# An FFT and two MLPs on one core: the steps from item 46 on in a new order, with subtractions split anew between VectorE and GpSimd

## The chip, the core and the metric

The kernel runs on one core of a Trainium2 chip. The metric is the time of one execution in device microseconds. The engines are named as a profile names them: PE (TensorE, the matrix engine, with PEld for its weight loads), DVE (VectorE), ACT (ScalarE), POOL (GpSimd) and SP (SyncE, which issues most DMAs). Each runs its own queue of instructions in order, and waits on semaphores for the others.

## What is computed

```python
X = np.fft.fft(np.fft.fft(x, axis=1), axis=2)      # x: 2 x 3008 x 256
x = X.real.reshape(6016, 256)
h = x @ w_in                                       # 256 x 2048
x = (h * np.clip(h + 3.0, 0.0, 6.0) / 6.0) @ w_out # 2048 x 256
xn = x / np.sqrt(np.mean(x * x, axis=-1, keepdims=True) + 1e-6) * rms_g
g = xn @ w_gate                                    # 256 x 1536
out = (g / (1 + np.exp(-g)) * (xn @ w_val)) @ w_out2   # 1536 x 256
```

All weights arrive as 64-bit floats, which the kernel decodes to 32 bits with integer operations.

## The kernel before

Every matrix product is made with operands split in two: `hi` is the 32-bit value rounded by ScalarE to the form that PE takes, `lo` is what is left, `f - hi`. A product is three passes (`PASSES`): hi x hi, and the two mixed ones. So each operand costs a copy on ScalarE and a subtraction, made by the helper `sub` (line 342). One helper for all of them means that all these subtractions have one line in the profile.

*First MLP.* The tokens are cut into six blocks of 2 x 502, the hidden units into 16 groups of 128; a block and a group make an **item**, 96 in all (`item1`). An item runs 6 matmuls into a pair of PSUM banks E and O (line 607, two pairs in turn), then on VectorE a multiply-add and two sums (lines 611, 613, 614), on ScalarE two ReLUs (619), on VectorE two multiplies (622), which read the banks for the last time, on ScalarE one rounding copy (625), two subtractions (342, `LO<-R,HI`), and 12 matmuls into four accumulators (640). The item two further on can start on the same pair of banks when line 622 has read them.

*Second MLP.* The same blocks, with 12 groups: 72 **chunks**. A chunk is seven products (`prod`, line 796, letters a to g in the order of steps), made by a scheme that saves one product in eight by sums and differences of the blocks of both operands; then on ScalarE copies from the bank (803), on VectorE sums with a bank (809), on ScalarE the SiLU (813), on VectorE the product of gate and value (817: of a tile with a bank, or of two tiles in SBUF, `R<-R,T`), a rounding copy (824), a subtraction (342), and the output matmuls (839).

*Work between.* While the first MLP runs, and into the second, the second MLP's weights are loaded (`load_w2`), decoded (`dec_w2`, lines 330 to 337: on VectorE two tensor_scalar and two operations on two tensors), summed (`sum_w2`, 711) and split (`split_w2`, 717 and 342). Each block is normalised (`rms`, 12 times): squares on ScalarE (739), their sum (742), a split, two matmuls with ones (751), a first guess by integer operations (755, 756), three Newton rounds (ScalarE 760, a product 762, VectorE 764) and two scalings (767). Its sums and differences (`sum_j`) and splits (`split_j`, 778) follow.

*The order.* It is written out by hand in one table, `STEPS` (from line 109 on). A word is a step: `47` is the next piece of item 47, `12d` the piece d of chunk 12, `rms5` the next piece of the sixth normalisation, and so on. Engines get their instructions in that order. Operations of `sub`, and lines 711, 742 and 762, go to GpSimd, and with an apostrophe behind the word to VectorE:

```python
        for step in STEPS.split():
            task = step.rstrip("'")
            low[0] = V if step != task else G
    def sub(o, a, b):
        low[0].tensor_tensor(o, a, b, op=ALU.subtract)
```

Of the kernel before, what the change touches and what calls it, by code (L numbers as in the profile page):

```python
# [132 lines left out]
    47 47 47 47 47 47 47 49 50 gr11 50 49 rms0 49 50 48 48 48 48 48 48 48 48 48 48 48 48 rms0 49' lo00 lo00 lo10 lo10 50  # L133
    gr11 rms0 gr11 gr11 gr11 gr11 rms0 pq11 51 51 50 pq11 pq11 pq11 pq11 pq11 rms0 51 49 49 49 49 49 49 49 49 rms0 51
    rms0 50 51 rms0 52 do00 50 rms0' 51 52 50 50 50 50 50 do10 52 51 52 rms0 51 52 53 rms0 rms0 53 52 51 51 51 51 53 52
    53 rms0 52 53 rms0 54 rms0 54 53 52 52 52 52 54 53 54 rms0 53 54 55 55 54 53 53 53 53 55 54 55 rms0 54 55 56 56 55
    54 54 54 54 56 55 56 do00 55 56 57 57 56 55 55 55 55 57 56 57 do00 56 do00 do00 58 57 hw07 lg00 lg00 56 56 56 56
    hw07 hw07 rms0 rms0 rms0 57 58 rms1 57 58 59 58 rms1 do10 58 dg00 57 57 57 57 57 rms1 59 58 rms1 59 59 rms1 58 do10
    59 rms1 58 58 58 58 58 rms1 59 do10 do10 rms1 59 60 dg00 lg10 lg10 hw08 60 rms1 61 60 60 59 59 59 59 59 rms1 60 hw08
    hw08 rms1 dg10 61 60 rms1 62 61 61 60 rms1 61 rms1 60 60 60 60 60 62 61 rms1 62 63 62 61 rms1 rms1 pq12 61 61 61 61  # L140
    61 rms1 rms1 rms1 62 pq12 pq12 pq12 pq12 pq12 63 64 62 63 62 hj00 63 64 62 62 62 62 62 63 hj01 hj00 hj00 64 63 65 64
    63 dg00 64 63 63 65 64 hj01 hj01 65 63 63 63 66 64 dg00 dg00 66 64 66 65 64 64 64 64 sj01 65 66 sj03 lv00 lv00 66 67
    65 hw00 65 67 68 66 67 65 65 65 65 65 hj04 68 66 68 67 66 66 66 66 66 67 dv00 hw00 hw00 dg10 67 dg10 68 69 67 dg10
    dg10 68 lv10 lv10 hw01 67 67 67 67 67 69 68 hw01 hw01 69 69 70 68 dv00 dv10 69 68 68 68 68 68 70 69 hj04 hj04 70 70
# [837 lines left out]
```

## Time and profile before

| | |
|---|---|
| median of 3 runs | 1093.73 us (1092.93 to 1095.08) |
| the profiled execution | 1095.86 us |
| its span, first to last instruction | 1094.1 us |
| PE busy | 1021.9 us (93%), 4356 matmuls recorded |
| DVE busy | 829.4 us (76%), 1202 instructions |
| ACT busy | 671.5 us (61%), 1081 |
| POOL busy | 616.1 us (56%), 500 |
| chain that ended last, by engine | PE 52%, DVE 37%, the rest 11% |
| mean granted clock of PE | 0.985 of 2.4 GHz |

The busy shares are means over stages with different limits. Matmuls are pipelined, so a matmul's own duration (some 390 ns) is longer than the time from its start to the next one's. The step at which the two orders part lies between items 47 and 51; item 50 starts at 289.1 us of the span, the second MLP's first output matmul at 519.1 us.

### The profile page before, as it was taken

What the parts mean: (1) busy time and instruction counts of PE and PEld (TensorE: products, weight loads), DVE (VectorE), ACT (ScalarE), POOL (GpSimd) and SP (SyncE); (2) the same over time, 40 slices, a digit from 0 to 9 for tenths busy, and PEclk for the clock granted to TensorE, in tenths of its full rate; (3) what the DMA queues carried; (4) which work ended last, traced back from release to release, by engine and by line L of the source; (5) the groups of instructions that cost most, each with busy time, mean ns of one, the idle gap of its engine ahead of it and who ended that gap; (6) DMA issues with size and microseconds to landing.
All of it is one profiled execution on the core that took longest, in us unless ns stands there. A gap on an engine that the chain in (4) does not pass through costs nothing.

```text
span 1094.1 us, 12459 instructions
## 1 busy us (share of the span) xinstructions
PE 1021.9 (93%) x4356; PEld 820.3 (75%) x4356; DVE 829.4 (76%) x1202; ACT 671.5 (61%) x1081; POOL 616.1 (56%) x500
## 2 busy tenths in 40 slices
PE   3879899999998899989988999999999999999997
PEld 2758777888875678768766777888788788878885
DVE  7998999987799999996798768556755755764443
ACT  5656556555656656666666666566566666755553
POOL 0057567666667869664656656636545753653332
PEclk9899999999999999999998999999999999999998
DMA  8450302043501110110130110110020011000001
GB/s 284 152 174 0 81 33 82 1 84 60 143 1 39 58 39 20 58 58 24 64 104 1 39 38 0 37 40 1 1 76 1 1 38 38 1 1 38 1 1 38
DMA packets 22118, 53.27 MB, mean 49 GB/s; under 512 B 4326, under 2 KB 9958, under 8 KB 21678
## 3 DMA queue, kind: packets, MB, share of 16 engines
q1 hardware_dynamic: 19320, 45.10, 12.5%
q0 software_dynamic: 2736, 7.38, 3.3%
q8 instruction: 34, 0.56, 0.2%
q14 instruction: 28, 0.23, 0.1%
HBM read 36.58 MB, written 11.32 MB: 44 GB/s over the span
## 4 chain that ended last, share of the span: by engine, by line
PE 52%; DVE 37%; issue 4%; ACT 3%; POOL 3%; DMA 1%; SPq 0%; POOLq 0%; DVEq 0%; ACTq 0%
PE E L796 13%; PE acc L839 13%; PE acc L640 10%; PE O L796 10%; DVE R L622 6%; DVE T L611 4%; DVE E L613 3%; DVE O L614 3%; PE E L607 2%; PE O L607 2%; DVE H L764 2%; DVE R L817 2%; DVE R L809 1%; DVE YB L335 1%; DMA J<-in_x 1%
## 5 line engine op out<-in xcount | busy, mean ns | idle before, releaser
L342 POOL TENSOR_TENSOR LO<-R,HI 128x502 fp32r<-128x502 f32 x191 | 246.1, 1313 | 132.5 <-ACT HI L625 128.5
L640 PE MATMUL acc<-HI,B 128*128 128x502 f32 x768 | 250.8, 392 | 0.6 <-ACT HI L625 0.3
L640 PEld LDWEIGHTS acc<-HI,B 128*128 128x128 f32 x768 | 145.7, 190 | 31.8 <-ACT HI L625 2.6
L640 PE MATMUL acc<-LO,B 128*128 128x502 f32 x384 | 153.6, 400 | 8.9 <-POOL LO L342 8.9
L342 POOL TENSOR_TENSOR HI<-R,HI 128x502 fp32r<-128x502 f32 x72 | 87.4, 1216 | 114.9 <-ACT HI L824 56.5
L625 ACT CAST HI<-R 128x1004 fp32r<-128x1004 f32 x96 | 99.2, 1036 | 85.6 <-DVE R L622 55.3
L809 DVE TENSOR_TENSOR R<-R,O 128x502 f32<-128x502 f32 x144 | 96.2, 674 | 49.6 <-PE O L796 39.3
L342 POOL TENSOR_TENSOR LO<-R,LO 128x502 fp32r<-128x502 f32 x68 | 82.6, 1218 | 87.8 <-ACT LO L824 48.3
L813 ACT ACTIVATE R<-R 128x502 f32<-128x502 f32 x144 | 89.7, 626 | 38.8 <-DVE R L809 38.2
L619 ACT ACTIVATE R<-E,c_three 128x502 f32<-128x502 f32 x96 | 65.3, 680 | 73.8 <-DVE E L613 59.4
L803 ACT COPY R<-E 128x502 f32<-128x502 f32 x144 | 83.0, 576 | 36.4 <-PE E L796 33.5
L607 PE MATMUL E<-J,A 128*128 128x502 f32 x288 | 84.9, 404 | 16.6 <-DVE R L622 13.8
L640 PEld LDWEIGHTS acc<-LO,B 128*128 128x128 f32 x384 | 72.9, 190 | 33.6 <-POOL LO L342 19.0
L809 DVE TENSOR_TENSOR T<-T,O 128x502 f32<-128x502 f32 x48 | 32.4, 675 | 71.6 <-ACT T L803 71.6
L607 PE MATMUL O<-J,A 128*128 128x502 f32 x288 | 83.4, 398 | 0.3 <-DVE A L390 0.3
L607 PEld LDWEIGHTS E<-J,A 128*128 128x128 f32 x288 | 54.6, 194 | 33.1 <-DVE R L622 19.6
L613 DVE TENSOR_TENSOR E<-T,O 128x502 f32<-128x502 f32 x96 | 65.6, 684 | 8.2
L622 DVE SCALAR_TENSOR_TENSOR R<-R,E 128x502 f32<-128x502 f32 x96 | 64.3, 669 | 3.6 <-ACT R L619 3.5
L614 DVE TENSOR_TENSOR O<-T,O 128x502 f32<-128x502 f32 x96 | 65.1, 678 | 0.0
L607 PEld LDWEIGHTS O<-J,A 128*128 128x128 f32 x288 | 55.5, 193 | 12.4 <-DVE A L390 0.7
L619 ACT ACTIVATE R<-O,c_three 128x502 f32<-128x502 f32 x96 | 64.7, 674 | 0.0
L622 DVE SCALAR_TENSOR_TENSOR R<-R,O 128x502 f32<-128x502 f32 x96 | 64.1, 668 | 0.0
(354 smaller groups left out, 2237.7 us busy)
## 6 DMA issues: line engine op xcount, KB each, us to landing
out_dram<-H SPq DMA_DIRECT2D x22, 251.0 KB, 2.0
y<-H SPq DMA_DIRECT2D x10, 502.0 KB, 2.8
W<-y SPq DMA_DIRECT2D x20, 251.0 KB, 2.8
A<-in_w_in SPq DMA_DIRECT2D x4, 1024.0 KB, 9.1
W<-in_w_out SPq DMA_DIRECT2D x6, 512.0 KB, 3.4
W<-in_w_gate SPq DMA_DIRECT2D x6, 512.0 KB, 3.5
W<-in_w_val SPq DMA_DIRECT2D x6, 512.0 KB
PQ<-in_x SPq DMA_DIRECT2D x3, 1008.0 KB
```

What stands on the lines that cost most here:

```text
L342: low[0].tensor_tensor(o, a, b, op=ALU.subtract)
L607: T.matmul(bk[:, :BL], a[:, lw, eo, fs], j[:, eo, lx], start=(n == 0), stop=(n == 2))
L613: V.tensor_tensor(E[:, :BL], t, O[:, :BL], op=ALU.add)
L614: V.tensor_tensor(O[:, :BL], t, O[:, :BL], op=ALU.subtract)
L619: S.activation(x, bk[:, :BL], AF.Relu, bias=c3)
L622: V.scalar_tensor_tensor(x, x, 6.0, bk[:, :BL], op0=ALU.min, op1=ALU.mult)
L625: S.copy(hi, r.rearrange("p (h n) -> p h n", h=2))
L640: T.matmul(acc[k][:, :BL], w[:, lw, f % 4, d * P:(d + 1) * P], (hi, lo)[lx][:, hf], start=(first and n == 0), stop=(last and n == 2))
L796: T.matmul(bk[:, :BL], w[:, lw, fs], j[:, lx], start=(n == 0 and m in (0, 1, 3)), stop=(n == 2), skip_group_check=True)
L809: V.tensor_tensor(c["t"][m], c["t"][m], c["b", 1][:, :BL], op=ALU.add)
L813: S.activation(t, t, AF.Silu)
L839: T.matmul(acc2[p, m][d][:, :BL], w[:, lw, cs], h[:, lx], start=(f == 0 and n == 0), stop=(f == NF2 - 1 and n == 2))
```

## The change

Only the table `STEPS` differs, and in it only the words from item 46's surroundings on; the words ahead of them are the same. The new words are the same steps in a new order, with apostrophes at other places. Two lines of the 109 that differ:

```diff
@@ -130,109 +130,109 @@
...
-    47 47 47 47 47 47 47 49 50 gr11 50 49 rms0 49 50 48 48 48 48 48 48 48 48 48 48 48 48 rms0 49' lo00 lo00 lo10 lo10 50
-    gr11 rms0 gr11 gr11 gr11 gr11 rms0 pq11 51 51 50 pq11 pq11 pq11 pq11 pq11 rms0 51 49 49 49 49 49 49 49 49 rms0 51
...
+    47 47 47 47 47 47 47 49 50 48 48 48 48 48 48 48 48 48 48 48 48 49 50 49 50 50 49 gr11 lo00 lo00 50 lo10 lo10 rms0 50
+    rms0' 51 gr11 50 rms0 gr11 gr11 gr11 gr11 pq11 49 49 49 49 49 49 49 49 rms0' 51 do00 pq11 pq11 pq11 pq11 pq11 51 51
...
```

In the built program every engine has the same operations as before, except that 76 instructions stand on VectorE's queue that stood on GpSimd's: 43 of line 342, 18 of line 762, 12 of line 742 and 3 of line 711.

What moved is seen at three places. First VectorE's queue in the first MLP, around item 73, where a part of `w_gate` is decoded into tile B (T, E, O and R are the item's tiles; X and c_wx its inputs; W the raw weights). Before:

```order
L611 SCALAR_TENSOR_TENSOR T_627_3357<-X_9_81,c_wx_77,E_624_3331 128x502
L613 TENSOR_TENSOR E_624_3331<-T_627_3357,O_625_3332 128x502
L614 TENSOR_TENSOR O_625_3332<-T_627_3357,O_625_3332 128x502
L332 TENSOR_SCALAR B_488_2559<-B_488_2559 128x512
L333 TENSOR_SCALAR B_488_2559<-B_488_2559 128x512
L622 SCALAR_TENSOR_TENSOR R_630_3365<-R_630_3365,E_624_3331 128x502
L622 SCALAR_TENSOR_TENSOR R_630_3365<-R_630_3365,O_625_3332 128x502
L611 SCALAR_TENSOR_TENSOR T_633_3393<-X_9_81,c_wx_77,E_631_3368 128x502
L613 TENSOR_TENSOR E_631_3368<-T_633_3393,O_632_3369 128x502
L614 TENSOR_TENSOR O_632_3369<-T_633_3393,O_632_3369 128x502
L335 SCALAR_TENSOR_TENSOR B_488_2559<-W_607_3230,B_488_2559 128x512
L622 SCALAR_TENSOR_TENSOR R_638_3409<-R_638_3409,E_631_3368 128x502
```

Now:

```order
L622 SCALAR_TENSOR_TENSOR R_620_3306<-R_620_3306,E_615_3277 128x502
L622 SCALAR_TENSOR_TENSOR R_620_3306<-R_620_3306,O_616_3278 128x502
L332 TENSOR_SCALAR B_483_2536<-B_483_2536 128x512
L333 TENSOR_SCALAR B_483_2536<-B_483_2536 128x512
L611 SCALAR_TENSOR_TENSOR T_624_3324<-X_9_81,c_wx_77,E_621_3312 128x502
L613 TENSOR_TENSOR E_621_3312<-T_624_3324,O_622_3313 128x502
L614 TENSOR_TENSOR O_622_3313<-T_624_3324,O_622_3313 128x502
L622 SCALAR_TENSOR_TENSOR R_626_3342<-R_626_3342,E_621_3312 128x502
L622 SCALAR_TENSOR_TENSOR R_626_3342<-R_626_3342,O_622_3313 128x502
L335 SCALAR_TENSOR_TENSOR B_483_2536<-W_595_3163,B_483_2536 128x512
L332 TENSOR_SCALAR B_483_2536<-B_483_2536 128x512
L333 TENSOR_SCALAR B_483_2536<-B_483_2536 128x512
```

Lines 332 and 333, and 335, stood between line 614 and the two lines 622 of the same item; they now stand behind the second line 622, ahead of line 611 of the next item.

Second, VectorE's queue in the second MLP's first chunks, where weights are decoded into tile YB (R, T and c_p are the chunks' tiles, E and O the banks, B and A the split weights). Before:

```order
L809 TENSOR_TENSOR T_824_4502<-T_824_4502,O_821_4472 128x502
L817 TENSOR_TENSOR R_823_4501<-R_823_4501,E_819_4459 128x502
L809 TENSOR_TENSOR R_828_4542<-R_828_4542,O_832_4555 128x502
L332 TENSOR_SCALAR YB_826_4515<-YB_826_4515 128x512
L333 TENSOR_SCALAR YB_826_4515<-YB_826_4515 128x512
L335 SCALAR_TENSOR_TENSOR YB_826_4515<-W_830_4547,YB_826_4515 128x512
L337 SCALAR_TENSOR_TENSOR YB_826_4515<-W_830_4547,YB_826_4515 128x512
L332 TENSOR_SCALAR YB_826_4515<-YB_826_4515 128x512
L333 TENSOR_SCALAR YB_826_4515<-YB_826_4515 128x512
L335 SCALAR_TENSOR_TENSOR YB_826_4515<-W_833_4570,YB_826_4515 128x512
L337 SCALAR_TENSOR_TENSOR YB_826_4515<-W_833_4570,YB_826_4515 128x512
L809 TENSOR_TENSOR R_823_4501<-R_823_4501,O_821_4472 128x502
```

Now:

```order
L809 TENSOR_TENSOR T_822_4474<-T_822_4474,O_825_4510 128x502
L817 TENSOR_TENSOR R_821_4473<-R_821_4473,E_820_4465 128x502
L337 SCALAR_TENSOR_TENSOR YB_823_4493<-W_813_4421,YB_823_4493 128x512
L809 TENSOR_TENSOR R_832_4567<-R_832_4567,O_831_4562 128x502
L332 TENSOR_SCALAR YB_823_4493<-YB_823_4493 128x512
L333 TENSOR_SCALAR YB_823_4493<-YB_823_4493 128x512
L809 TENSOR_TENSOR R_821_4473<-R_821_4473,O_825_4510 128x502
L335 SCALAR_TENSOR_TENSOR YB_823_4493<-W_827_4538,YB_823_4493 128x512
L342 TENSOR_TENSOR B_828_4540<-YB_823_4493,B_828_4540 128x512
L337 SCALAR_TENSOR_TENSOR YB_823_4493<-W_827_4538,YB_823_4493 128x512
L817 TENSOR_TENSOR R_821_4473<-R_821_4473,T_822_4474 128x502
L332 TENSOR_SCALAR YB_823_4493<-YB_823_4493 128x512
```

The four decoding operations stood in runs of four and eight; they now stand singly or in pairs between the chunks' lines 809 and 817, with a weight's subtraction (342) among them that was on GpSimd.

Third, a normalisation in the second MLP's steady part (H holds the value and its inverse root, HI the product of a Newton round). Before, GpSimd's queue:

```order
L342 TENSOR_TENSOR PQ_567_3023<-H_1025_6136,PQ_567_3023 128x502
L342 TENSOR_TENSOR LO_1027_6173<-R_1016_6060,LO_1027_6173 128x502
L342 TENSOR_TENSOR LO_1031_6203<-R_1016_6060,LO_1031_6203 128x502
L342 TENSOR_TENSOR PQ_567_3023<-W_974_5750,PQ_567_3023 128x502
L762 TENSOR_TENSOR HI_1030_6196<-HI_1030_6196,H_1025_6136 128x502
L342 TENSOR_TENSOR HI_1034_6230<-R_1022_6130,HI_1034_6230 128x502
L762 TENSOR_TENSOR HI_1030_6196<-HI_1030_6196,H_1025_6136 128x502
L342 TENSOR_TENSOR HI_1037_6261<-R_1022_6130,HI_1037_6261 128x502
L342 TENSOR_TENSOR W_974_5750<-W_976_5778,W_974_5750 128x502
```

Now the rounds on VectorE's queue:

```order
L756 TENSOR_SCALAR H_1019_6107<-H_1019_6107 128x502
L762 TENSOR_TENSOR HI_1030_6198<-HI_1030_6198,H_1019_6107 128x502
L809 TENSOR_TENSOR T_1025_6142<-T_1025_6142,O_1023_6130 128x502
L764 SCALAR_TENSOR_TENSOR H_1019_6107<-HI_1030_6198,H_1019_6107 128x502
L809 TENSOR_TENSOR R_1033_6214<-R_1033_6214,O_1032_6208 128x502
L762 TENSOR_TENSOR HI_1030_6198<-HI_1030_6198,H_1019_6107 128x502
L817 TENSOR_TENSOR R_1024_6141<-R_1024_6141,E_1022_6123 128x502
L764 SCALAR_TENSOR_TENSOR H_1019_6107<-HI_1030_6198,H_1019_6107 128x502
L809 TENSOR_TENSOR R_1024_6141<-R_1024_6141,O_1023_6130 128x502
L762 TENSOR_TENSOR HI_1030_6198<-HI_1030_6198,H_1019_6107 128x502
L817 TENSOR_TENSOR R_1024_6141<-R_1024_6141,T_1025_6142 128x502
L764 SCALAR_TENSOR_TENSOR H_1019_6107<-HI_1030_6198,H_1019_6107 128x502
```

Two of this normalisation's three products (762) stood on GpSimd, whose result line 764 on VectorE takes; now all three stand on VectorE.

## Rows read from the trace of the kernel before

**Rows 1.** Four stretches: us, busy us (instructions) by engine, granted clock, DMA share, GB/s

```profile
289.10:519.10 230.00, 215.48 (x914) 168.36 (x913) 213.46 (x311) 146.39 (x212) 161.52 (x125) 1.00 0.13 44
519.10:632.00 112.90, 101.23 (x410) 78.01 (x409) 93.40 (x119) 71.70 (x131) 70.89 (x54) 0.95 0.17 56
632.00:1004.40 372.40, 367.32 (x1592) 297.71 (x1592) 231.35 (x315) 239.65 (x429) 202.22 (x168) 1.00 0.06 20
1004.40:1094.10 89.70, 83.46 (x358) 67.43 (x356) 37.96 (x58) 44.56 (x77) 26.96 (x23) 0.96 0.05 18
```

**Rows 2.** The same view: a piece of the first stretch, and one without waits

```profile
300.00:400.00 100.00, 89.68 (x372) 67.80 (x371) 97.64 (x135) 60.56 (x88) 74.13 (x58) 1.00 0.10 32
...
1000.00:1050.00 50.00, 50.00 (x222) 41.37 (x221) 23.69 (x36) 28.04 (x49) 15.41 (x13) 1.00 0.03 11
```

**Rows 3.** Single lines on VectorE: count, shortest/median/longest ns, first and last start

```profile
L764 DVE SCALAR_TENSOR_TENSOR H<-HI,H x30: 667/682/1754, 580.8 to 958.9; 128x502 f32<-128x502 f32 x30
...
L622 DVE SCALAR_TENSOR_TENSOR R<-R,E x96: 659/670/680, 54.9 to 504.1; 128x502 f32<-128x502 f32 x96
...
L335 DVE SCALAR_TENSOR_TENSOR YB<-W,YB x12: 682/694/1740, 455.9 to 566.0; 128x512 int32<-128x512 int32 x12
...
L333 DVE TENSOR_SCALAR YB<-YB x12: 426/427/1490, 455.4 to 565.1; 128x512 int32<-128x512 int32 x12
```

**Rows 4.** Order of time, VectorE then GpSimd: start us, us, instruction, idle time before

```profile
317.87 0.68 DVE L614 TENSOR_TENSOR O<-T,O 128x502 f32<-128x502 f32 x1
318.45 1.15 DVE L767 SCALAR_TENSOR_TENSOR YB<-YB,c_gn,HI 128x502 f32<-128x502 f32 x1
...
342.86 0.68 DVE L337 SCALAR_TENSOR_TENSOR B<-W,B 128x512 int32<-128x512 int32 x1
343.46 1.50 DVE L332 TENSOR_SCALAR B<-B 128x512 f32<-128x512 f32 x1
...
317.79 2.75 POOL L342 TENSOR_TENSOR LO<-R,HI 128x502 fp32r<-128x502 f32 x2 [1.50 <-ACT HI L625]
...
343.30 1.38 POOL L342 TENSOR_TENSOR LO<-R,HI 128x502 fp32r<-128x502 f32 x1 [1.39 <-ACT HI L625]
```

**Rows 5.** Groups on VectorE, 289.1 to 519.1: count, busy us, mean ns

```profile
L337 DVE SCALAR_TENSOR_TENSOR B<-W,B 128x512 int32<-128x512 int32 x6 | 7.6, 1267 | 0.1
L764 DVE SCALAR_TENSOR_TENSOR HI<-R,HI 128x502 f32<-128x502 f32 x6 | 6.8, 1131 | 0.0
L767 DVE SCALAR_TENSOR_TENSOR YB<-YB,c_gn,HI 128x502 f32<-128x502 f32 x4 | 6.6, 1670 | 0.0
L335 DVE SCALAR_TENSOR_TENSOR B<-W,B 128x512 int32<-128x512 int32 x6 | 6.6, 1100 | 0.0
L333 DVE TENSOR_SCALAR B<-B 128x512 int32<-128x512 int32 x6 | 6.5, 1088 | 0.2
L332 DVE TENSOR_SCALAR B<-B 128x512 f32<-128x512 f32 x6 | 5.6, 932 | 0.0
```

**Rows 6.** Order of time: VectorE from 357.61, TensorE's wait at 362.23

```profile
357.61 3.98 DVE L767 SCALAR_TENSOR_TENSOR YB<-YB,c_gn,HI 128x502 f32<-128x502 f32 x2
...
362.23 0.96 PE L607 MATMUL E<-J,A 128*128 128x502 f32 x3 [2.26 <-DVE R L622]
```

**Rows 7.** Order of time, TensorE, 554 to 561 us

```profile
554.15 0.85 PE L796 MATMUL E<-J,B 128*128 128x502 f32 x3
...
558.12 1.17 PE L796 MATMUL O<-PQ,A 128*128 128x502 f32 x3 [2.44 <-DVE R L809]
559.08 1.46 PE L796 MATMUL O<-B,B 128*128 128x502 f32 x3
```

**Rows 8.** Groups on VectorE, 632.0 to 1004.4; then TensorE at 774.90 us

```profile
L817 DVE TENSOR_TENSOR R<-R,T 128x502 f32<-128x502 f32 x33 | 28.3, 861 | 16.2 <-ACT R L813 15.7
L764 DVE SCALAR_TENSOR_TENSOR H<-HI,H 128x502 f32<-128x502 f32 x24 | 26.5, 1106 | 7.0 <-POOL HI L762 6.4
...
774.90 0.95 PE L796 MATMUL O<-YB,B 128*128 128x502 f32 x3 [0.49 <-DVE T L809]
```

More of the change, by code (lines that the diff above doesn't have):

```diff
@@ new lines @@
+    dv12 dv12 6u hw25 rms2 ly1 ly1 7e rms2 hw25' hw25 6w 7l rms2 sw21' rms2 7f sw23' hw23 8a sw22' hw24 8b hw23' hw23
+    hw22 sw24' 8h hw22' hw22 hw26 8c hw24' hw24 8k hw26' hw26 8e rms2' 7m 8l rms2 7g 7n rms2 8f 7o 7r rms2 9a 8i 7p 9b
+    9h 7q 8d 8j 7s 9i 7t 9c 8m 9j 7v 7u 8n 9k 8r rms2 7w 8s rms2 rms2' 8g rms2 9d 8o 9e rms2 8p 8v rms2 rms2 rms2 9l
+    hj10 8q 9f rms3 9m hj10 hj10 10a 9n 8t 9g rms3' 9r 8u 10b 10h 9o rms3 10c 10i 9s 9p 8w 10j rms3' 10k 9q rms3 hj11
+    10d rms3 hj11' hj11 10e 9t rms3 9v 10l 9u rms3 10m 10f rms3' 9w rms3 10n rms3 10g 10r rms3' 11a 10s 10o 11b 10p rms3
@@ new lines @@
+    10v 11h 10q rms3 11i 10t rms3 11c 11j 11d 11k 10u 12a 10w rms3 12h rms3 rms3 rms3 rms3 11e sj11' 12b hj16 sj13' 11l
+    hj13 hj16' hj16 11f hj14 11m hj13 hj13 11n 11g hj14' hj14 11r 13a 11o sj12 13h 12i 13b 11s 11p 12d hj12 13i 12j 11v
+    sj14' 13j hj12' hj12 hj15 11q 12c ev0o0 hj15' hj15 11t 13c ev0o0 ev0o0 12k ly2 11u 13d ly2 ly2 13k 12e 11w 12l 12m
+    ev0o0 ev0o0 12f 12g 12n 13e 12o 12r 14a 12p 12s 14b 13l 14h 12q 13f ev0o1 13m 12v 12t ev0o1 ev0o1 12u 13n 13g 14i
+    13r 12w 13o 14j 13s 13p ev0o1 ev0o1 14c 13q 14d 13t 13v 14k 13u rms4 13w rms4' 14e rms4 15a 14l rms4' 15b 15h 14m
@@ new lines @@
+    24j 22v 22u 23o 23r 23p 23s 22w 23q 24c 23t 24d 24k 23u 23v ev1o0 23w ev1o0 ev1o0 24e 25a 24l 25b 24m 25h ev1o0
+    ev1o0 24f 25i 24g 24n 25j 25c 24o 24r 25d 24p 24s 26a ev1o1 25k 24q 24v ev1o1 26h ev1o1 24t 25e 24u 26c 25l 24w 25m
+    ev1o1 ev1o1 26k 25f 25g 25n 26b 25o 25r 26e rms6 26i 25s 27a 25p rms6' 26d 26j 25q 25v rms6 25t rms6' 26l 25u 27b
+    27h 26m 26f 27i 25w 26n 27j 26r 26g 26s 27c 26o 27d 26p rms6 27k 26q 26v rms6 26t rms6 27e 26u rms6 28a 27l rms6'
+    26w 28h 27m rms6 27f rms6 27g 27n rms6 28c 27o 27r 28b 27p 27s 29a 28k 28i 28e rms6 28j 27q 28d 29h rms6 27v 27t
@@ new lines @@
+    32n 32g 31u hj32 32r 33b 32o sj34 33h 31w 32p 33i 32s 33j 33c 32q 33d 33k hj32' hj32 32t 32v 32u 33e 32w 33l 33m 33f
+    33g 33n 34a 33o 33r 34b 33p 33s 35a 34h 33q 34c 35h 34i 33v 33t 34k 33u 34j 34d hj34 33w hj34' hj34 34e 35c 34l 35b
+    34m 35k hj36 34f 35i hj35 hj36 hj36 34g 34n 35j 35d 34o 34r hj35 hj35 35e 34p 36a 34s ly4 35l ly4 ly4 36b 35m 36h
+    35f 34q 36i 35g 34t 35n 36j 34v 34u 35o 35r 35p 35s 34w 35q 36c 35t 36d 36k 35u 35v ev2o0 35w ev2o0 ev2o0 36e 37a
+    36l 37b 36m 37h ev2o0 ev2o0 36f 37i 36g 36n 37j 37c 36o 36r 37d 36p 36s 38a ev2o1 37k 36q 36v ev2o1 38h ev2o1 36t
@@ new lines @@
+    41o 42d 41p rms9 42k 41q 41v hj41 rms9 hj41' hj41 41t rms9 42e 43a 41u rms9 43b 42l rms9' 43h 41w 42m rms9 43i 42f
+    rms9 43j 42g rms9' 42n 43c rms9 42r 43d 42o 43k 42s 44a rms9 43e 42p rms9' 44h 42v 42q 43l rms9 42t 43f 43m 42u 44c
+    43n 42w rms9 43r 44k rms9 rms9 rms9 43s 43g 44b 43o 44e sj41' 43p 43v 44i hj43 sj43 44l 43q 44j 44d hj43' hj43 43t
+    44f 44m sj42 45a 44n 44g 43u hj42 44r 45b 44o sj44 45h 43w 44p 45i 44s 45j 45c 44q 45d 45k hj42' hj42 44t 44v 44u
+    45e 44w 45l 45m 45f 45g 45n 46a 45o 45r 46b 45p 45s 47a 46h 45q 46c 47h 46i 45v 45t 46k 45u 46j 46d hj44 45w hj44'
@@ L236 @@
+    71q 71t ev5o0 71u ev5o0 ev5o0 71w ev5o1 ev5o0 ev5o0 ev5o1 ev5o1 ev5o1 ev5o1
 """
```

176 lines of the change are left out of this document (75 added, 101 removed).

## The prediction

> **What bounds the kernel now.** I read the stretches first, then what the engines wait for, then the order of the instructions.
>
> The span after item 50 falls into four stretches, one row each [rows 1]: the rest of the first MLP (289.1 to 519.1 us), the first twelve chunks of the second MLP with the last of the weight decoding (519.1 to 632.0), its steady part (632.0 to 1004.4) and the end. Where nothing holds TensorE up it runs 222 matmuls in 50.00 us [rows 2], 0.2252 us each. At that pace the four stretches need 914 x 0.2252 = 205.8, 410 x 0.2252 = 92.3, 1592 x 0.2252 = 358.5 and 358 x 0.2252 = 80.6 us. They took 230.0, 112.9, 372.4 and 89.7. So 24.2, 20.6, 13.9 and 9.1 us are waiting, 68 us in all; no reordering can give back more than that.
>
> In the first stretch the engine that sets the pace is VectorE: 97.64 busy of 100 us in one piece of it [rows 2], where PE stands at 89.68. Part of that busy time is no work. A multiply that takes one operand from PSUM (L622) lasts 659 to 680 ns whatever else runs. An operation with both inputs in SBUF lasts 667 ns at its shortest, but up to 1754 (L764); L335 goes from 682 to 1740, and L333, a tensor_scalar from SBUF to SBUF, from 426 to 1490 [rows 3]. The rows in order of time say when: the L767 of 318.45 takes 1.15 us while GpSimd works on two low-word subtractions from 317.79 on; the L337 of 342.86, which GpSimd does not meet, takes 0.68, and the L332 behind it, which runs into the GpSimd subtraction of 343.30, takes 1.50 [rows 4]. In the first stretch six groups carry most of this [rows 5]. Against the shortest durations, and about 0.7 for L767, it is 6 x 0.585 + 6 x 0.464 + 4 x 0.95 + 6 x 0.418 + 6 x 0.66 + 6 x 0.51 = 19.6 us; with the smaller groups of the same view some 27. The same sum gives some 24 us in the second stretch and 32 in the third.
>
> What it costs TensorE is seen where the slow instruction stands between the sum that ends an item's pre-activation (L614) and the multiply that frees its PSUM banks (L622). Two L767 at 357.61 took 3.98 us there, and TensorE waited 2.26 us for that L622 [rows 6].
>
> **The change part by part.** It is a permutation: the same 4358 matmuls, 1083 ScalarE and 113 SyncE instructions. 76 instructions leave GpSimd for VectorE: 43 subtractions (L342), 18 products (L762), 12 sums (L742) and 3 sums (L711), counted in the two orders. By stretch that is 3, 25 and 48.
>
> *Their price.* A VectorE instruction follows the one before by 0.6 us (317.87 to 318.45) [rows 4], so 2, 15 and 29 us of VectorE. On GpSimd they took some 1.3 us each (2.75 for two [rows 4]); GpSimd has room either way.
>
> *First stretch.* Of the runs of SBUF-only operations between items on VectorE, 30 of 41 stood right behind an L614 before, which is when GpSimd subtracts for the item ahead [rows 4]; now 14 of 42 do, 23 stand right behind the second L622, where GpSimd still waits for ScalarE's rounding, and 5 elsewhere. I take half of the 27 us as gone, since half of the runs have left the place where they collide: 13.5 us, less 2 for the three added, plus something for the L622s that are no longer held. **-13 us.** Ends: -24, when TensorE runs at its pace throughout, and 0, when the new places collide as the old ones did. If this stall goes, the next late thing is TensorE itself; the margin left is 11 us.
>
> *Second stretch.* VectorE is busy 93.4 of 112.9 us [rows 1]: 69.7 of work, 23.7 of collision. With 15 added it has 84.7 of work against TensorE's 92.3. GpSimd is busy 70.9 us, 63% of the stretch; without 25 operations of 1.3 it has 39, 37% of some 105. Collisions in proportion to that, on 93 exposed operations where 68 were, are 23.7 x 37/63 x 93/68 = 19 us. The order also avoids some, as in the first stretch; I take 13. VectorE then needs 98. It stood idle for 19.5 us, mostly behind chunks whose own sums it had delayed: it ran decoding in runs of eight, and TensorE waited 2.44 us for an L809 behind one. After that wait the matmuls ran at the lower of the clock's two levels, 1.2 GHz: 1.46 us for three from 559.08 on, where three took 0.85 before [rows 7], so 0.6 us lost on each such group; the granted clock of the stretch is 0.95 [rows 1]. The new order deals the decoding out in ones and twos between the chunk's operations; I leave 8 us idle. 98 + 8 = 106, **-7 us.** Ends: -20 (TensorE's pace), and +15, if the collisions stay at 24 and the idle time at 19.5 (84.7 + 24 + 19.5 = 128).
>
> *Third stretch.* Here VectorE has room: 231.4 of 372.4 us, 260 with the 29. The waits are short and come with each normalisation: L764, the last step of a Newton round, at 1106 ns where it needs 667, 24 times; the product with both inputs in SBUF at 861, 33 times; and TensorE's wait for the L809 behind them, 0.49 us at 774.90 [rows 8], which comes back in each two blocks. In a Newton round the product (L762) used to cross to GpSimd and back; now it stands on VectorE in most rounds and GpSimd is not in the chain. I take a little under half of the 13.9 us. **-6 us.** Ends: -14, and +5 if each of five normalisations gains a new wait of 1 us because VectorE has become the later engine.
>
> *End.* The last chunks' subtractions stay on GpSimd, and its low words are the last thing the final matmuls wait for. **0**, ends -1 and +1.
>
> *DMAs.* The weight loads and the reloads of the first MLP's output move with their steps on SyncE's queue, each still a few items or chunk operations ahead of its first reader; none of the waits named here goes to such a load. 0.
>
> The sum is -26 us against the profiled execution's 1095.86: 1069.9. That execution stands 2.1 us above the median of the runs, 1093.73, so the forecast for the median is **1068 us**.
>
> One rule of the Trainium skill goes further than the rows. "SBUF — State Buffer", section Who interferes with whom, has the two engines' shared port pair as an exclusive lock that whoever starts first holds for the whole instruction. The durations in rows 3 and 4 agree with it. By that rule alone a right order avoids every collision, all 83 us of VectorE time would go, and the sum would be the low ends, -59 us, near 1036. I don't take it, since 14 of 42 runs still stand at the old place.
>
> **Rivals.**
>
> *A. VectorE becomes the bound in the second stretch (slower).* It gets 25 more operations just where decoding, splitting and the chunks meet. If each of the 93 exposed operations collides as the 68 do now (23.7 / 68 = 0.35 us), that is 32 us, and 84.7 + 32 + 8 = 125, +12. An order that is wrong about the collisions there is wrong elsewhere: -6 in the first stretch, +4 in the third. Sum +10, 1104 us. It decides from the point at which collisions there pass 112.9 - 84.7 - 8 = 20 us. For it: VectorE is the fullest engine behind TensorE. Against it: GpSimd has half as much to collide with. Chance 0.14.
>
> The Trainium skill speaks for A: "Perfetto Trace Analysis", section Optimizing Scalar/DVE Operations, would move work off a saturated VectorE, even to GpSimd, which is the reverse of this change; it adds that between these two engines it might not help.
>
> *B. The change doesn't do what it says.* The places on VectorE are new, but GpSimd's turn shifts with them, and each collision is met one item later. Then only what is moved counts, the 2 to 3 us of both signs cancel, and the time is 1093. For it: queues run free of any clock, so that an order only fixes who follows whom on one engine. Against it: the place behind L622 is tied to GpSimd's wait by data, not by timing. Chance 0.06.
>
> *C. Only the first stretch gains.* 13 us there, nothing elsewhere: 1081. For it: VectorE is nearly full in the second stretch before and after. Chance 0.15, and the forecast's case has 0.65.
>
> **How the numbers follow.** A measurement of this kernel tells 0.2% (2.2 us) from no change. Faster by more: forecast and C, 0.80. Within 0.2%: B, 0.06. Slower: A, 0.14. The range holds the forecast and C: its low end, 1050, is the forecast with three quarters of the way to the low ends in the first two stretches (0.75 x 24 = 18), its high end, 1090, is C with the second and third stretches worse by 9 together. It leaves out A, and half of B's case.
>
> **What would show it.** Right: in the first stretch L335, L337 and L764 at means under 0.9 us, DVE's busy share near 0.95 with PE at 0.96 or more, and a length of 214 to 220 us; in the second stretch GpSimd busy about 40 us and no piece at the lower clock; in the third a PE wait of under 1 us in each two blocks. Wrong: VectorE over 98 busy of the second stretch's length with PE waiting for L809 or L817; or L764 and L337 at their old means, which is B.

## The result, and the profile after

The changed kernel takes **1066.24 us** (median of 4 runs, 1064.86 to 1067.67), the kernel before 1094.40 in the same comparison: a ratio of 0.9744, 95% interval 0.9726 to 0.9763, 2.6% faster. The forecast was 1068 and the range 1050 to 1090.

The same stretches as in [rows 1], in the trace after (us, then busy us and instructions of PE, PEld, DVE, ACT and POOL, granted clock, DMA share, GB/s):

```profile
286.90:502.20 215.30, 209.80 (x912) 170.28 (x911) 197.13 (x314) 145.28 (x213) 149.05 (x120) 1.00 0.14 45
502.20:605.90 103.70, 99.03 (x411) 76.25 (x410) 91.78 (x142) 72.48 (x131) 38.84 (x30) 0.98 0.20 64
605.90:972.80 366.90, 365.90 (x1593) 297.43 (x1591) 243.80 (x364) 236.04 (x427) 141.04 (x120) 1.00 0.06 20
972.80:1063.80 91.00, 84.30 (x361) 66.80 (x359) 43.34 (x58) 44.66 (x78) 27.12 (x24) 0.99 0.05 18
```

The span went from 1094.1 to 1063.8, 30.3 us: 14.7 in the first stretch, 9.2 in the second, 5.5 in the third, -1.3 in the end, and 2.2 ahead of item 50. That last one is not the change's: the steps there are the same, and in the runs below that leave them as they are they took between 285.8 and 289.6.

VectorE has 76 instructions more and is no busier, 829.7 us where it was 829.4. The groups of [rows 5], on VectorE in the first stretch after (count, busy us, mean ns, idle time before):

```profile
L335 DVE SCALAR_TENSOR_TENSOR B<-W,B 128x512 int32<-128x512 int32 x6 | 4.2, 701 | 0.0
L337 DVE SCALAR_TENSOR_TENSOR B<-W,B 128x512 int32<-128x512 int32 x6 | 4.2, 700 | 0.0
L764 DVE SCALAR_TENSOR_TENSOR HI<-R,HI 128x502 f32<-128x502 f32 x6 | 4.1, 675 | 0.0
...
L333 DVE TENSOR_SCALAR B<-B 128x512 int32<-128x512 int32 x6 | 2.6, 428 | 0.2
L332 DVE TENSOR_SCALAR B<-B 128x512 f32<-128x512 f32 x6 | 2.5, 420 | 0.0
```

L337 went from 1267 ns to 700, L764 from 1131 to 675, L333 from 1088 to 428, close to the shortest times of [rows 3].

Adding up what every VectorE instruction with all its operands in SBUF (the lines listed below, 755, 756, and 817 with two tiles) takes above its clean duration (L764 676 ns, L335 and L337 691, L333 427, L332 418 and so on for the other lines) gives the **excess** of a stretch, the measure used from here on. It fell from 27.9 to 8.8 us in the first stretch, from 23.6 to 8.8 in the second, from 32.3 to 16.8 in the third; in the end it rose from 0.1 to 4.9.

Why it fell is seen where the two engines meet. For the SBUF-only instructions of VectorE in the first stretch (lines 332, 333, 335, 337, 342, 711, 742, 762, 764, 767), I asked whether a GpSimd instruction ran alongside, and which of the two had started first. "Long" is over 0.1 us above the shortest of the same line and shape in the run:

| | no GpSimd alongside | VectorE first | GpSimd first |
|---|---|---|---|
| before | 11, 0 long | 6, 0 long | 46, 44 long, 26.0 us above |
| after | 27, 0 long | 13, 0 long | 28, 16 long, 7.4 us above |

Where VectorE starts first, it isn't slowed. Where GpSimd is first, VectorE's instruction ends only after GpSimd's. Before, in order of time, VectorE and then GpSimd:

```profile
404.08 0.82 DVE L332 TENSOR_SCALAR B<-B 128x512 f32<-128x512 f32 x1
404.94 1.18 DVE L333 TENSOR_SCALAR B<-B 128x512 int32<-128x512 int32 x1
...
403.35 2.49 POOL L342 TENSOR_TENSOR LO<-R,HI 128x502 fp32r<-128x502 f32 x2 [1.44 <-ACT HI L625]
```

GpSimd's two subtractions end at about 404.6 and at 405.84. L332 ends at 404.90 and L333 at 406.12, each some 0.28 us behind one of them. An L337 of 0.68 us, met in the same way, ends 0.55 us behind GpSimd's first:

```profile
413.41 1.09 DVE L337 SCALAR_TENSOR_TENSOR B<-W,B 128x512 int32<-128x512 int32 x1
...
412.67 2.76 POOL L342 TENSOR_TENSOR LO<-R,HI 128x502 fp32r<-128x502 f32 x2 [1.44 <-ACT HI L625]
```

In each case that is the instruction's own length less some 0.14 us: nearly all of it runs after GpSimd is done. The same rows show the other direction. GpSimd's second subtractions, which start while L332 and L337 run, end at 405.84 and 415.43, 0.94 and 0.93 us behind them. So a collision delays the low words too. After the change the same pair of lines, behind the second L622:

```profile
386.62 0.42 DVE L332 TENSOR_SCALAR B<-B 128x512 f32<-128x512 f32 x1
387.07 0.43 DVE L333 TENSOR_SCALAR B<-B 128x512 int32<-128x512 int32 x1
...
385.57 1.07 POOL L342 TENSOR_TENSOR LO<-R,HI 128x502 fp32r<-128x502 f32 x1
387.90 1.27 POOL L342 TENSOR_TENSOR LO<-R,HI 128x502 fp32r<-128x502 f32 x1 [1.26 <-ACT HI L625]
```

The subtraction of 385.57 ends at 386.64, just as L332 starts; the next one waits for ScalarE's rounding until 387.90. Both fit between. In 28 cases GpSimd is still first, but in 13 of them VectorE starts in the last 0.12 us of GpSimd's instruction, and 12 of these are not long.

TensorE's waits in the first stretch, before and then after (what it waited for: us in total, times, longest), show what reached it:

```profile
PE acc L640 <- POOL LO L342: 8.9, 12, 0.9
PE E L607 <- DVE R L622: 4.9, 5, 2.3
```

```profile
PE acc L640 <- POOL LO L342: 3.8, 7, 0.8
PE E L796 <- DVE R L622: 0.5, 1, 0.5
```

The larger part is the wait for GpSimd's low words, the smaller one the wait for a bank; both shrank.

### The profile page after: what moved, and what is told of

It reads as the page before. It is cut to its first block, busy times and chain, and to the rows that moved or that the text cites. A ratio compares the mean times of both kernels' runs of the same rounds, so it can differ in the third digit from the quotient of the medians.

```text
span 1063.8 us, 12508 instructions
## 1 busy us (share of the span) xinstructions
PE 1010.9 (95%) x4356; PEld 817.9 (77%) x4356; DVE 829.7 (78%) x1278; ACT 667.7 (63%) x1081; POOL 510.0 (48%) x424
## 4 chain that ended last, share of the span: by engine, by line
PE 63%; DVE 23%; ACT 4%; issue 4%; DMA 2%; POOL 2%; SPq 0%; POOLq 0%; DVEq 0%; ACTq 0%
PE E L796 17%; PE acc L839 16%; PE O L796 12%; PE acc L640 11%; DVE R L622 5%; DVE T L611 3%; PE E L607 3%; DVE E L613 3%; PE O L607 2%; DVE O L614 2%; POOL LO L342 1%; DMA J<-in_x 1%; DVE B L342 1%; ACT R L619 1%; ACT HI L625 1%
## 5 line engine op out<-in xcount | busy, mean ns | idle before, releaser
L342 POOL TENSOR_TENSOR LO<-R,HI 128x502 fp32r<-128x502 f32 x192 | 240.8, 1277 | 125.3 <-ACT HI L625 125.3
L640 PE MATMUL acc<-LO,B 128*128 128x502 f32 x384 | 151.0, 393 | 3.8 <-POOL LO L342 3.8
L342 POOL TENSOR_TENSOR LO<-R,LO 128x502 fp32r<-128x502 f32 x72 | 88.2, 1225 | 127.4 <-ACT LO L824 58.9
L809 DVE TENSOR_TENSOR R<-R,O 128x502 f32<-128x502 f32 x144 | 96.3, 674 | 31.1 <-PE O L796 25.8
L803 ACT COPY R<-E 128x502 f32<-128x502 f32 x144 | 82.0, 573 | 16.1 <-PE E L796 11.6
L809 DVE TENSOR_TENSOR T<-T,O 128x502 f32<-128x502 f32 x48 | 32.3, 673 | 54.8 <-ACT T L803 53.1
L824 ACT CAST LO<-R 128x502 fp32r<-128x502 f32 x72 | 44.1, 612 | 46.5 <-DVE R L817 46.1
L622 DVE SCALAR_TENSOR_TENSOR R<-R,E 128x502 f32<-128x502 f32 x96 | 64.5, 672 | 8.9 <-ACT R L619 8.8
L614 DVE TENSOR_TENSOR O<-T,O 128x502 f32<-128x502 f32 x96 | 65.1, 678 | 0.0
```

Of the source, the lines that this page charges most:

```text
L614: V.tensor_tensor(O[:, :BL], t, O[:, :BL], op=ALU.subtract)
L622: V.scalar_tensor_tensor(x, x, 6.0, bk[:, :BL], op0=ALU.min, op1=ALU.mult)
L640: T.matmul(acc[k][:, :BL], w[:, lw, f % 4, d * P:(d + 1) * P], (hi, lo)[lx][:, hf], start=(first and n == 0), stop=(last and n == 2))
L809: V.tensor_tensor(c["t"][m], c["t"][m], c["b", 1][:, :BL], op=ALU.add)
```

## The experiments

**Theory:** the time went with the collisions, which the new places and the new split both avoid. **Rival "split":** the 76 moved instructions do it alone. **Rival "order":** the new order does it alone.

### The order alone, and the split alone

`e1_order_only`: the new order, with each step's apostrophe as before.

```diff
-49 50 50 49 gr11 ... lo10 rms0 50 rms0' 51 gr11 ... 63 66 sj01' 64
+49 50 50 49' gr11 ... lo10 rms0 50 rms0 51 gr11 ... 63 66 sj01 64
```

> The new order with the old split: each step keeps its new place, and its apostrophe is that of before. Theory 1 (collisions of SBUF-only operations on VectorE with GpSimd's, lessened both by the places and by the moved instructions): the first stretch keeps most of its gain, 215 to 220 us; the second and the third, where GpSimd has its 73 instructions back, lose theirs, 110 to 116 and 370 to 375; total 1075 to 1085. Rival 2 (the gain is the split's: a slow GpSimd operation replaced by a fast one in the chains, wherever it stands): 1090 or more. Rival 3 (the gain is the order's alone, TensorE's groups above all): 1065 to 1070.

`e2_split_only`: the old order, with each step's apostrophe as after.

```diff
-48 rms0 49' lo00 ... gr11 rms0 pq11 ... 64 sj01 65 ... 69 hj04 hj04
+48 rms0' 49 lo00 ... gr11 rms0' pq11 ... 64 sj01' 65 ... 69 hj04' hj04
```

> The old order with the new split. Theory 1: the first stretch stays at 226 to 232 us, since the decoding stands where it collided; the second gains little, 108 to 115, with VectorE fuller and the decoding still in runs; the third gains 2 to 6; total 1083 to 1095. Rival 2 (split alone): 1066 to 1070. Rival 3 (order alone): 1092 to 1097.

| | median us | ratio to before (95%) | first | second | third |
|---|---|---|---|---|---|
| before | 1095.42 | | 230.0 | 112.9 | 372.4 |
| order alone | 1103.18 | 1.006 (1.004 to 1.008) | 216.5 | 119.2 | 384.5 |
| split alone | 1093.70 | 0.9981 (0.9968 to 0.9993) | 232.8 | 112.6 | 369.8 |
| both: the change | 1066.24 | 0.9744 (0.9726 to 0.9763) | 215.3 | 103.7 | 366.9 |

(The change was timed beside 1094.40 us.) Neither rival holds. The first stretch's gain is the order's. In the second and third the order alone makes it slower, by 6 and 12 us, the split alone gives 0 and 3, and both together give 9 and 6. The parts don't add up; each needs the other. The theory's own ranges for the order alone held in the first stretch and missed in the second, the third and the total: I had expected the lost split to cost a gain, not to cause a loss. For the split alone they held, but for 0.8 us in the first stretch.

The excess doesn't price the second and the third stretch. With the split alone it fell from 23.6 to 14.8 us and from 32.3 to 20.9, and they gained 0.3 and 2.6; with the order alone it fell to 20.1 and 28.7, and they lost. There the waits between the engines count as well.

What the order lacks without the split is read from VectorE's waits, order alone, second stretch (engine, line, what it waited for: us in total, times, longest):

```profile
DVE H L764 <- POOL HI L762: 6.3, 4, 2.7
...
DVE YB L711 <- POOL YB L711: 4.9, 1, 4.9
```

That is 11.2 us at the head of VectorE's queue for results that GpSimd still owes (before: 4.1 and 1.2 in the same view). The order puts such a step's successor right behind it, as if VectorE itself made the result. The split alone fails in the other way: VectorE is busy 98.5 of the 112.6 us, still with its decoding in runs of four and eight, and TensorE waits some 13 us.

### Which part of the split

`e6_rms_back`: the change, with the normalisations' steps on the engines of before (41 instructions go back to GpSimd net). `e9_splits_back`: the change, with the splits and sums of the weights (hw, sw) and of the blocks (hj, sj) as before (40 net). The 76 are net too: 89 steps go to VectorE and 13 come back; five of these 13 are subtractions of an item and of chunks, which both runs leave as in the change.

```diff
 e6_rms_back
-rms0 50 rms0' 51 ... 5w 6p rms2' 7j
+rms0 50 rms0 51 ... 5w 6p rms2 7j
 e9_splits_back
-63 66 sj01' 64 ... 87 hw06 hw06 ... 88 hw02' hw02
+63 66 sj01 64 ... 87 hw06' hw06 ... 88 hw02 hw02
```

> The changed order, with the normalisations' subtractions, sums and products (L342, L742, L762 in the rms steps) on the engines they had before; the weights' splits (hj, hw, sj, sw) stay as in the change. Chain theory (what the new order lacks without the new split is the normalisation's Newton rounds staying on VectorE, since each product that crosses to GpSimd and back now falls on a moment at which GpSimd is taken): the third stretch gets back most of what the order alone lost, 378 to 384 us where the change took 366.9, the second stretch stays near the change's 103.7 (102 to 107), total 1079 to 1088. Count theory (only the number of operations on GpSimd matters, wherever they come from; some half of the moved ones go back): half of the loss of the order alone in each stretch, 111 in the second and 376 in the third, total near 1084. The second stretch tells the two apart.

> The changed order, with the weights' splits and sums (the apostrophes of hj, hw, sj, sw) as before the change, and the normalisations as in the change: the complement of the run before it. Chain theory: the third stretch stays near the change's (366 to 371), the second loses nearly all that the order alone lost there (114 to 119 us), total 1077 to 1085. Count theory: again half of the loss in each, 111 and 376, total near 1084.

| | ratio to before (95%) | second, of it POOL busy | third, of it POOL busy |
|---|---|---|---|
| the change | 0.9744 (0.9726 to 0.9763) | 103.7, 38.8 | 366.9, 141.0 |
| normalisations back | 0.9865 (0.985 to 0.988) | 110.3, 48.2 | 375.4, 177.9 |
| splits back | 0.9922 (0.9904 to 0.994) | 116.6, 64.9 | 370.9, 166.1 |
| both back (order alone) | 1.006 (1.004 to 1.008) | 119.2, 69.0 | 384.5, 202.0 |

The chain theory missed with the normalisations back: the second stretch lost 6.6 us, not up to 3, and the third 8.5, under its 11 to 17. With the splits back both stretches lie in its ranges, and the total of 1087.56 us above its 1085. The count theory's 111 and 376 came with the normalisations back (110.3 and 375.4), not with the splits back (116.6 and 370.9), since I had spread the steps evenly over the two stretches. Counted by stretch, a larger loss goes with more of GpSimd's time in both: 6.6 us for 9.4 more and 12.9 for 26.0 in the second; 8.5 for 36.8 and 4.0 for 25.0 in the third. A normalisation step costs somewhat more than a split step in each, which leaves the chain a share of it that these runs don't price.

The splits' price has a place of its own. Splits back, order of time, GpSimd, VectorE, TensorE:

```profile
519.09 1.29 POOL L342 TENSOR_TENSOR B<-YB,B 128x512 fp32r<-128x512 f32 x1 [1.37 <-ACT B L717]
520.46 2.64 POOL L711 TENSOR_TENSOR YB<-YB 128x512 f32<-128x512 f32 x2
...
523.13 1.74 DVE L711 TENSOR_TENSOR YB<-YB 128x512 f32<-128x512 f32 x1 [4.85 <-POOL YB L711]
524.79 0.67 DVE L809 TENSOR_TENSOR c_p<-c_p,O 128x502 f32<-128x502 f32 x1
...
525.51 1.62 PE L796 MATMUL O<-B,YB 128*128 128x502 f32 x3 [3.56 <-DVE c_p L809]
```

VectorE's L711 stands 4.85 us behind two sums on GpSimd; the L809 that frees a bank stands behind it, and TensorE waits 3.56. In the change all three sums are VectorE's, 3.25 us in a row, and TensorE waits 1.77 there. With the normalisations back it is the chunk's own splits that come late, third stretch, TensorE's waits:

```profile
PE acc L839 <- POOL HI L342: 4.1, 8, 0.7
PE acc L839 <- POOL LO L342: 1.9, 6, 0.5
```

After the change that view has 0.7 us once for HI, and none for LO.

### The place in the first stretch

`e3_place_before`: the kernel before, with the runs of SBUF-only operations that stood behind L614 moved behind the second L622 of the same item (35 of 37 runs stand there). `e5_place_back`: the change, with the runs moved behind the next L614 (30 of 34).

```diff
 e3_place_before
-49 rms0 51 rms0 50 51 rms0 52 do00 ... 52 51 52 rms0 51 52 53
+49 rms0 51 50 51 rms0 rms0 52 do00 ... 52 51 52 51 52 rms0 53
 e5_place_back
-rms0 50 rms0' 51 gr11 50 rms0 gr11 gr11 gr11 gr11 pq11 49 49 49
+rms0 50 51 50 49 49 ... 49 49 51 51 rms0' gr11 rms0 gr11
```

> The kernel before, with one thing changed in the first stretch: a run of SBUF-only operations behind line 614 is moved behind the next line 622, so that 35 of 37 runs stand there and one behind line 614; old split, and all else in the old order. Theory 1: the durations above the clean ones in that stretch fall from 27 us to under 14, its length from 230 to between 217 and 222, total 1082 to 1088. Rival 2 and rival 3: no change, 1092 to 1096.

> The changed kernel, with one thing undone in the first stretch: a run of SBUF-only operations behind line 622 is moved behind the next item's line 614, so that 30 of 34 runs stand there; new split, all else in the new order. Theory 1: the collisions come back, 9 us of them now and 18 to 30 then, and the first stretch goes from 215 to between 222 and 230; total 1073 to 1081. Rivals 2 and 3: within 2 us of 1066.

| | ratio to before (95%) | first stretch | its excess | GpSimd first: long, us above |
|---|---|---|---|---|
| before | | 230.0 | 27.9 | 46: 44, 26.0 |
| before, runs behind L622 | 0.9988 (0.9973 to 1.0003) | 229.3 | 16.1 | 27: 22, 15.7 |
| the change | 0.9744 (0.9726 to 0.9763) | 215.3 | 8.8 | 28: 16, 7.4 |
| the change, runs behind L614 | 0.9931 (0.991 to 0.9952) | 237.6 | 19.7 | 31: 30, 19.3 |

Moving the place alone took 12 us of excess away and gave less than 1 us, where the theory had 217 to 222; the time is the one that the rivals expected. VectorE was busy 204.1 us where it was 213.5 before, but idle 25.2 where it was 16.5. Where the rest went is in VectorE's wait for ScalarE's ReLU between L614 and L622, here with the place alone moved (count, busy us, mean ns, idle time before and what ended it):

```profile
L622 DVE SCALAR_TENSOR_TENSOR R<-R,E 128x502 f32<-128x502 f32 x47 | 31.8, 676 | 9.5 <-ACT R L619 9.1 <-POOL LO L342 0.5
```

Before, this group waits 0.8 us in all, after the change 6.2. A run that stood behind L614 filled the time in which the ReLU was under way; with the runs gone VectorE stands there, 0.2 to 0.3 us an item. In the change the 25 items with nothing between L614 and L622 wait 6.2 us, the 22 others nothing. TensorE's granted clock also was 0.98 in this stretch, where it was 1.00 before: behind a wait of 1.82 us for an L622 three matmuls took 1.62 us from 348.75 on, where three took 0.84 ahead of it. What that cost was not separated.

The change is a middle way: what it leaves behind L614 are 14 runs of 10.3 us of clean work, 13 of them of one instruction, where before there were 30 of 24.5 us, up to 2.1 each. That the sizes rather than the moment within GpSimd's work make the difference between 16.1 and 8.8 was not tried by itself. The change with its runs behind L614 is the slowest there, above the 222 to 230 expected. Its moved runs came together in pieces of up to 3.7 us, so it mixes place and size. It waits 9.5 us for the ReLU as well, 1.24 to 1.27 us at each of five items that do have a run behind L614; why was not tried.

### GpSimd's inputs

`e7_write_only`: the kernel before, with the first MLP's low words written as zeros, which leaves them out of the product (GpSimd reads nothing, but also works 0.5 us instead of 1.3 and no longer waits for ScalarE). `e10_one_input`: the same with a product of the rounded word with zero, one input, waiting as before. `e11_write_only_after`: the first edit in the changed kernel.

```diff
-            sub(lo[:, x], rh[x], f32(hi[:, x]))
+            G.memset(f32(lo[:, x]), 0.0)
+            G.tensor_scalar(lo[:, x], f32(hi[:, x]), 0.0, None, op0=ALU.mult)
```

(one of the two lines with the plus, for the steps that stand on GpSimd)

> The order and split of before. In the first MLP's items GpSimd's subtraction that makes the low word is replaced by writing zeros into the same tile (so the low word of the hidden values is left out of the product): GpSimd reads nothing there, at the same place of its queue. Theory (VectorE's long instructions in the first stretch are collisions with those subtractions): VectorE's time above its clean durations in the first stretch falls from 27.9 us to under 8, and the stretch from 230 to 208 to 216 us. Rival (they are long because of GpSimd's writes, or of something else at that place, such as the ReLU of ScalarE): still over 20 us above the clean durations, stretch over 224 us.

> The order and split of before. In the first MLP's items GpSimd's subtraction is replaced by a product of the rounded word with zero: it still waits for ScalarE's rounding and stands at the same place of the queue, but reads one input, not two (the low word of the hidden values is left out). Theory (it is the place in time, tied to the rounding, that makes VectorE's long instructions, and any GpSimd work with an SBUF input there collides): VectorE's time above its clean durations stays above 15 us in the first stretch, and the stretch above 222 us. Rival (only two-input operations on GpSimd hold the port): under 8 us, 208 to 214 us.

> The changed order and split with GpSimd's subtraction in the first MLP's items replaced by writing zeros (low word of the hidden values left out), as in the run of before with that edit, whose first stretch took 211.4 us. Theory (the new order's gain of 14.8 us in the first stretch is wholly the collisions it avoids, so without them the order is worth nothing there): 208 to 212 us, within 3 us of the old order's. Rival (the new order is also better in itself, by where it puts work between an item's steps): 5 us or more under 211.4.

Each of the three was run once (1072.10, 1081.45 and 1054.43 us). The first stretch of before with writes only, of before with one input, of the change with writes only (columns as in the first fence):

```profile
283.90:495.40 211.50, 208.81 (x915) 171.24 (x915) 192.30 (x309) 145.56 (x212) 86.51 (x125) 1.00 0.15 48
```

```profile
287.90:506.40 218.50, 212.23 (x915) 169.25 (x914) 197.49 (x310) 146.19 (x212) 182.33 (x126) 1.00 0.14 46
```

```profile
282.60:491.80 209.20, 207.40 (x912) 170.94 (x911) 189.52 (x312) 144.81 (x213) 79.78 (x120) 1.00 0.14 47
```

With writes only the old order runs at 211.5 us and the new one at 209.2, with excess 6.8 and 1.3. So of the 14.7 us between the two orders 2.3 are left once those subtractions don't read: most of the gain of the first stretch is the avoided collisions, as the theory had it in these two runs. Both stand within 6 us of TensorE's pace of 205.8 us, though, so a gain of another kind could be hidden there. The one-input run lies between both its expectations: 218.5 us and an excess of 11.5, though GpSimd is busy 182 us in it, more than the 161.5 of [rows 1]. Of 44 VectorE instructions that met a low-word subtraction in before 36 were long, by 19.7 us; of 52 that met the one-input product 23, by 7.3 us; of 14 that met a write 1, by 0.3 (by the GpSimd instruction met first). So it is mostly the two-input read that holds VectorE, not how long GpSimd is busy; the place decides how often the two meet.

### Beating both

`e4_tail`: the change, with the last chunk's two low-word subtractions on VectorE. `e8_tail_2m`: that, and steps 2l and 2m ahead in the second stretch.

```diff
 e4_tail
-71n 71o 71r 71s 71p 71v ... 71t ev5o0 71u ev5o0
+71n 71o 71r 71s' 71p 71v ... 71t ev5o0 71u' ev5o0
 e8_tail_2m, besides
-hw15 2e sw11' 3c 2l sw13' hw13 3b sw12' hw14 2f 2m hw13
+hw15 2e 2l sw11' 2m 3c sw13' hw13 3b sw12' hw14 2f hw13
```

> The change, with the last chunk's two low-word subtractions (71s and 71u) on VectorE. In the change's trace TensorE waits 0.84 and 0.66 us for GpSimd's low words at the end, and one L817 collides with them. Theory: 0.6 to 1.2 us less than the change's 1066.24. Rival: VectorE's own sums are then later by the same, no difference within 0.3 us.

> The run before it, and in the second stretch the chunk steps 2l and 2m moved ahead, around sw11', so that VectorE's three sums of weights (L711, 3.25 us in a row in the change's trace) no longer stand ahead of the L809 for which TensorE waits 2.15 us. Theory: up to 2 us less than the run before it. Rival: the weights' sums are then needed sooner than they come, or the wait moves to the next chunk's L809, no difference within 0.5 us.

TensorE's last waits, the change and then `e4_tail`:

```profile
1056.23 1.73 PE L839 MATMUL acc<-LO,B 128*128 128x502 f32 x6 [0.84 <-POOL LO L342]
1058.62 1.39 PE L839 MATMUL acc<-LO,B 128*128 128x502 f32 x5 [0.66 <-POOL LO L342]
```

```profile
1053.18 1.87 PE L839 MATMUL acc<-LO,B 128*128 128x502 f32 x6 [0.23 <-DVE LO L342]
1055.27 1.40 PE L839 MATMUL acc<-LO,B 128*128 128x502 f32 x5 [0.22 <-DVE LO L342]
```

Both waits shrank and the end took 90.1 us where it took 91.0, as expected. The whole kernel gives 1066.00 us and a ratio of 0.9725 (0.9705 to 0.9745): 0.9 us doesn't show beside an unchanged beginning that varies by more. `e8_tail_2m` removed the wait of 1.77 us, and its second stretch took 102.2 us where `e4_tail`'s took 102.3; the whole 1065.99, 0.9726 (0.9707 to 0.9744). Neither is shown to beat the change.

## Why the prediction was right

The time, its sign and the order of its terms came out. By its steps:

- **First stretch, -13, measured -14.7.** L335, L337 and L764 came to 701, 700 and 675 ns, the length of 215.3 lies in the 214 to 220 given, PE is at 0.97 of it. DVE's share, though, is 0.92 and not 0.95. The step that was off is "I take half of the 27 us as gone, since half of the runs have left the place": 19 of 28 us went, while a term that it left out, VectorE's wait for the ReLU, grew by 5.4. That the two errors partly cancel is luck. The reason doesn't stand by itself either, as moving the runs alone gained under 1 us; what decides is which engine starts first, and the time that VectorE stands at the ReLU. The cost was shown as a wait for a bank; the larger wait of TensorE was the one for GpSimd's low words, 8.9 us of 14.1.
- **Second stretch, -7, measured -9.2.** GpSimd is busy 38.8 us, forecast 39. VectorE is busy 91.8 where 98 was forecast, 4.2 us of it because 13 us of collision were taken and 8.8 came; it is idle 11.9 where 8 was forecast. These two misses point opposite ways and partly cancel, which is luck. That collisions are the price of this stretch isn't shown: the split alone lowered them by 8.8 us and gained 0.3. "No piece at the lower clock" was wrong: one place is left, behind a wait for ScalarE, where before there were two:

```profile
559.49 1.61 PE L796 MATMUL E<-PQ,B 128*128 128x502 f32 x3 [0.67 <-ACT R L803]
560.90 1.46 PE L796 MATMUL O<-B,B 128*128 128x502 f32 x3
```

- **Third stretch, -6, measured -5.5.** TensorE's waits there fell from 5.1 to 1.0 us in all. Of the two groups in [rows 8] only L764 got shorter, from 1106 ns to 672; L817 stayed, so a good part of the collisions between the chunks' own steps is still there (VectorE in the third stretch, after):

```profile
L817 DVE TENSOR_TENSOR R<-R,T 128x502 f32<-128x502 f32 x32 | 28.2, 881 | 6.2 <-ACT R L813 6.2
...
L764 DVE SCALAR_TENSOR_TENSOR H<-HI,H 128x502 f32<-128x502 f32 x24 | 16.1, 672 | 0.0
```

- **End, 0, measured +1.3**, just outside its ±1. The excess there rose by 4.8 us, and TensorE's waits from 2.5 to 3.0; with the low words on VectorE, in `e4_tail`, the end took 90.1 us. What the 1.3 us consist of was not separated.
- **What was wrong in the reasoning:** the terms of the order and of the split were added as if each had its own price. The order alone showed -13.5 us in the first stretch and +6.3 and +12.1 in the others. Rival A, VectorE as the bound, doesn't arise in the change; a slower kernel of another make does, the new order without its split, where VectorE waits for GpSimd instead. Rival B is refuted by the table of who is first: collisions didn't shift by one item, 19 of 28 us of them went. Rival C is refuted by the 9.2 and 5.5 us of the second and third stretch.

Two rules were weighed. "SBUF — State Buffer", section Who interferes with whom, of the Trainium skill, says that the port goes as an exclusive lock to whoever comes first; the 19 VectorE-first cases, none of them long, and the held instructions that run after GpSimd's agree. The one-input product of the experiment does not quite: it held VectorE's two-input instructions for a part of its time only. That a right order would avoid them all did not come: 39 of 84 us of excess remain. "Perfetto Trace Analysis", section Optimizing Scalar/DVE Operations, says that taking work off a saturated VectorE, even onto GpSimd, may make sense, and adds that between these two it might not help; here the two runs that do so lose 1.2 and 1.8 hundredths of the time to the change. VectorE isn't saturated there, 88% busy in the second stretch of the change and 66% in the third.

## What to carry to other kernels

When an instruction takes 1.2 us in one place and 0.7 in another, line up the two engines' rows in time before counting busy shares: a busy engine may be waiting inside its instructions. An order and a split are one decision: each place in an in-order queue assumes which engine makes the operand ahead, so try them together, and price them by stretch. Moving work out of a collision pays only as far as the gap that it filled has no wait of its own.

## What was not expected of the hardware

How many inputs GpSimd's instruction reads matters more than how long it takes. The one-input product of the experiment, and the subtraction of before, GpSimd in the first stretch:

```profile
L629 POOL TENSOR_SCALAR LO<-HI 128x502 fp32r<-128x502 f32 x94 | 142.3, 1532 | 26.2 <-ACT HI L625 23.6 <-PE O L510 2.4
```

```profile
L342 POOL TENSOR_TENSOR LO<-R,HI 128x502 fp32r<-128x502 f32 x93 | 119.9, 1310 | 52.1 <-ACT HI L625 48.1 <-issue 3.5 <-PE acc L640 0.4
```

The first is the longer one, and lengthened VectorE's instructions by 7.3 us over 52 meetings; the second by 19.7 over 44. The rows in order of time tell when. A VectorE instruction with two SBUF inputs that met the subtraction and was long ended 0.54 to 0.55 us behind it, all 26 of them; the 11 that were long beside the product ended 0.32 to 0.34 us before it did. So the product held them during its first part alone. A tensor_scalar (L332, L333) ended 0.59 us before the product five times, and 0.28 us behind it, as behind a subtraction, seven times. Beside a write none of 10 two-input instructions was long, and one of four tensor_scalars. Why the parts of GpSimd's instruction differ so was not tried.
